# Attention with transposed scores, head pairs and interleaved FFN groups in place of row-max attention followed by a separate FFN stage

## The chip, the core and the metric

The kernel runs on one core of a Trainium2 chip. The metric is the device time of one execution in microseconds (us). The engines are named as the profile names them: PE (matrix multiply), PEld (its weight loads, which overlap PE), DVE (vector), ACT (activation functions), POOL (general purpose; here it also issues DMAs and writes masks) and SP (issues DMAs). SBUF is the memory on the core, PSUM the banks that PE writes, DRAM the memory outside.

## The reference, cut to what matters

```python
# q, k, v: (8 batches, 8 heads, 576, 64); beacon_k, beacon_v: (8, 8, 16, 64)
k_all = concatenate([beacon_k, k], axis=2)          # 592 keys; the 16 beacons are never masked
v_all = concatenate([beacon_v, v], axis=2)
scores = (1 / sqrt(64)) * q @ k_all^T               # causal mask over the 576 ordinary keys
scores = scores - scores.max(-1, keepdims=True)
a = exp(scores); a /= a.sum(-1, keepdims=True) + 1e-9
attn = a @ v_all
x = attn.transpose(0, 2, 1, 3).reshape(4608, 512)   # heads side by side
out = (maximum(x @ w_gate, 0) * (x @ w_val)) @ w_out     # d_ff = 1536, float32 out
```

Apart from the 1e-9, subtracting the row maximum changes no result in exact arithmetic. It only keeps `exp` in range.

## The kernel before

Attention runs for one head at a time and one tile of 128 queries at a time. Scores have queries on the partitions, so the probabilities `p` have to be transposed tile by tile on PE, and copied back by ACT, before they can be multiplied by the values. The result goes to DRAM, and a second stage, the FFN, reads it back.

```python
for b in range(B):
    for h in range(H):
        ...                                     # load k, q, v; transpose k and q on PE; ACT copies them
        for qi in range(n_sq):                  # tiles of 128 queries
            while c0 < sk_cols:
                nc.tensor.matmul(sps[:rl, :cl], qT, kT[:, c0:c0 + cl], start=True, stop=True)
                nc.vector.tensor_copy(sc[:rl, c0:c0 + cl], sps[:rl, :cl])
            nc.gpsimd.affine_select(...)        # causal mask with -1e9
            nc.vector.reduce_max(row_max[:rl], sc[:rl, :sk_cols], axis=AX.X)
            nc.scalar.mul(neg_max[:rl], row_max[:rl], -1.0 * scale)
            nc.scalar.activation(p[:rl, :sk_cols], sc[:rl, :sk_cols], AF.Exp,
                                 bias=neg_max[:rl], scale=scale, accum_out=row_sum[:rl])
            nc.vector.reciprocal(rinv[:rl], row_sum[:rl])
            nc.vector.tensor_scalar_mul(p[:rl, :sk_cols], p[:rl, :sk_cols], rinv[:rl])
            for ci, (vt16, clen) in enumerate(v_chunks[:1 + n_need]):
                nc.tensor.transpose(ptp[:clen, :rl], p[:rl, col_off:col_off + clen], ident[:rl, :rl])
                nc.scalar.copy(ptile[:clen, :rl], ptp[:clen, :rl])
                nc.tensor.matmul(outp[:, :rl], vt16[:clen], ptile[:clen, :rl], ...)
            nc.vector.tensor_copy(ot[:, :rl], outp[:, :rl])
            nc.sync.dma_start(xT_dram[...], ot[:, :rl])
...                                             # second stage: load and cast the weights
for mi in range(n_m):                           # 9 tiles of 512 tokens
    ...                                         # load xT_f from xT_dram, cast to bf16
    for nf in range(NF):                        # 12 up groups: 4 gate and 4 value matmuls of 512 columns
        ...
    for ms in range(M_TILE // P):               # 4 down groups: 12 matmuls of 512 columns
        ...
```

## Time and profile before

The time is 1340.23 us, the median of two runs (1339.97 and 1340.49).

| | stage | us | PE busy us |
|---|---|---|---|
| attention | 0 to 1043 | 1043 | 820 |
| weights arrive, first FFN tile starts | 1043 to 1110 | 67 | 60 |
| rest of the FFN | 1110 to 1339 | 229 | 225 |

The first fence holds lines of the page of the kernel before: the busy time of each engine (us, share of the span, instructions), PE's busy tenths and the granted PE clock in 40 equal slices, and the chain of work that ended last, by engine.

```profile
PE 1104.7 (83%) x5008; PEld 509.3 (38%) x5008; DVE 725.4 (54%) x2268; ACT 733.4 (55%) x3053; POOL 97.2 (7%) x326
...
PE   6878888787788788888878877887874699999998
...
PEclk9999999999999999999999999999999899999999
...
PE 63%; ACT 17%; DVE 10%; issue 5%; DMA 2%; POOL 1%; SPq 1%; ACTq 0%; POOLq 0%; DVEq 0%
```

No engine is full during attention (the first 31 slices); PE comes nearest. The chain goes mostly through PE, with ACT and DVE steps between. The next fence, from the page's list of costliest groups, shows two of these steps. Its columns are line, engine, operation, output and input, shapes, count, busy us, mean ns of one, and idle time before it with the releaser.

```profile
L139 ACT COPY ptile<-ptp 128x128 bf16<-128x128 bf16 (+4 forms) x1280 | 301.4, 244 | 229.8 <-PE ptp L135 208.3
L135 PE MATMUL ptp<-ident,p 128*128 128x128 bf16 (+4 forms) x1280 | 325.1, 268 | 24.6 <-DVE p L129 22.9
```

The transposes of `p` are 1280 matmuls, and ACT spends 301 us copying them. The next fence is the timeline of PE in attention, then at the start of the FFN, then late in the FFN. Its columns are start us, duration us, engine, line, operation, output and inputs, array rows*columns in use, input shape, count.

```profile
303.80 0.32 PE L140 MATMUL outp<-ptile,kqv_5144 128*64 128x128 bf16 x1
304.05 0.29 PE L135 MATMUL ptp<-ident,p 128*128 128x128 bf16 x1
304.26 0.32 PE L84 MATMUL tp_5427<-ident,kqv_5425 128*64 128x128 bf16 x1
304.37 0.31 PE L87 MATMUL tp_5430<-ident,kqv_5425 128*64 128x128 bf16 x1
304.48 0.31 PE L140 MATMUL outp<-ptile,kqv_5156 128*64 128x128 bf16 x1
...
1044.68 5.62 PE L184 MATMUL gps<-xT_r,wg_r 128*128 128x512 bf16 x17
...
1150.24 1.03 PE L184 MATMUL gps<-xT_r,wg_r 128*128 128x512 bf16 x4
1151.10 1.03 PE L187 MATMUL vps<-xT_r,wv_r 128*128 128x512 bf16 x4
```

Two things are to be read here, from the starts and not from the durations, since ends are modelled. First, matmuls of the same array shape (128*64) start 0.11 us apart (304.26, 304.37, 304.48), while a change of shape costs 0.21 to 0.25 us (303.80 to 304.05 to 304.26). Of the 3711 pairs of consecutive attention matmuls in the trace, 2947 change shape. Second, late in the FFN four 512-column matmuls take 0.86 us (1150.24 to 1151.10), so 216 ns each, or 0.42 ns per column; the first FFN matmuls, after a pause, start 427 ns apart until 1048.4. In attention the spacing of `sps` matmuls grows by about 0.84 ns per column (226 ns at 144 columns, 332 at 272, 441 at 400). That is half speed, although the clock row says 9.

### The profile page before, as it was taken

The numbers are of one execution on the slowest core, as the hardware profiler recorded it, in microseconds if no ns is written. First come the engines' busy times: TensorE is split into PE (matmuls) and PEld (weight loads), VectorE is DVE, ScalarE is ACT, GpSimd is POOL, SyncE is SP. The second block draws the span as 40 slices with busy tenths as digits, with TensorE's granted clock in tenths as the row PEclk, the third lists the DMA queues.
The fourth block names the chain that finished last, engine by engine and source line by source line (L and its number), as shares of the span: only waits on it lengthen the run. The fifth ranks groups of instructions, "written<-read, shape, count | busy, mean of one in ns | idle before, by whom it ended". The sixth has DMA issues, their size and how long they took to land.

```text
span 1338.8 us, 20191 instructions
## 1 busy us (share of the span) xinstructions
PE 1104.7 (83%) x5008; PEld 509.3 (38%) x5008; DVE 725.4 (54%) x2268; ACT 733.4 (55%) x3053; POOL 97.2 (7%) x326
## 2 busy tenths in 40 slices
PE   6878888787788788888878877887874699999998
PEld 2333333333333333333333333333332244444443
DVE  4656566565556556656655565665564443433333
ACT  5666666666666666666666666666663122222222
POOL 0101000010000100000000010010000000000000
PEclk9999999999999999999999999999999899999999
DMA  1111111111111111111111111111116711101111
GB/s 41 41 39 38 38 39 38 39 39 37 40 40 39 39 38 38 38 39 41 38 39 40 39 38 38 38 38 38 41 37 223 263 64 63 64 34 38 40 40 40
DMA packets 168311, 67.97 MB, mean 51 GB/s; under 512 B 140032, under 2 KB 156416, under 8 KB 168192
## 3 DMA queue, kind: packets, MB, share of 16 engines
q1 hardware_dynamic: 168192, 66.68, 18.9%
q8 instruction: 39, 0.64, 0.2%
q14 instruction: 80, 0.66, 0.2%
HBM read 47.71 MB, written 18.87 MB: 50 GB/s over the span
## 4 chain that ended last, share of the span: by engine, by line
PE 63%; ACT 17%; DVE 10%; issue 5%; DMA 2%; POOL 1%; SPq 1%; ACTq 0%; POOLq 0%; DVEq 0%
PE ptp L135 14%; PE outp L140 14%; PE sps L103 9%; ACT p L124 8%; PE vps L187 7%; PE ops L196 7%; PE gps L184 7%; ACT ptile L139 5%; DVE row_max L119 3%; DVE sc L105 3%; ACT kT L85 2%; DVE ot L145 1%; ACT qTall L88 1%; DVE p L129 1%; POOL sc L108 1%
## 5 line engine op out<-in xcount | busy, mean ns | idle before, releaser
L139 ACT COPY ptile<-ptp 128x128 bf16<-128x128 bf16 (+4 forms) x1280 | 301.4, 244 | 229.8 <-PE ptp L135 208.3
L135 PE MATMUL ptp<-ident,p 128*128 128x128 bf16 (+4 forms) x1280 | 325.1, 268 | 24.6 <-DVE p L129 22.9
L105 DVE COPY sc<-sps 128x144 f32<-128x144 f32 (+6 forms) x448 | 194.0, 438 | 159.8 <-PE sps L103 157.2
L135 PEld LDWEIGHTS <-p 128*128 128x128 bf16 (+4 forms) x1280 | 127.4, 100 | 231.5 <-issue 64.7
L124 ACT ACTIVATE p<-sc,neg_max 128x144 bf16<-128x144 f32 (+4 forms) x320 | 197.7, 618 | 18.8 <-ACT neg_max L121 1.1
L103 PE MATMUL sps<-kT,qTall 64*128 64x144 bf16 (+6 forms) x448 | 170.5, 420 | 39.1 <-ACT qTall L88 35.5
L119 DVE TENSOR_REDUCE row_max<-sc 128x1 f32<-128x144 f32 (+4 forms) x320 | 176.3, 551 | 47.1 <-POOL sc L108 42.5
L190 ACT ACTIVATE g<-gps 128x512 f32<-128x512 f32 x108 | 64.5, 597 | 235.0 <-PE gps L184 223.4
L108 POOL TENSOR_SCALAR_AFFINE_SELECT sc<-sc 128x128 f32<-128x128 f32 (+1 forms) x320 | 96.5, 301 | 921.5 <-DVE sc L105 528.5
L145 DVE COPY ot<-outp 64x128 f32<-64x128 f32 (+1 forms) x320 | 84.7, 265 | 97.3 <-PE outp L140 95.9
L191 DVE TENSOR_TENSOR hT_r<-g,vps 128x512 bf16<-128x512 f32 x108 | 74.2, 688 | 108.9 <-PE vps L187 108.9
L184 PE MATMUL gps<-xT_r,wg_r 128*128 128x512 bf16 x432 | 112.4, 386 | 18.1 <-DVE wg_r L169 18.1
L187 PE MATMUL vps<-xT_r,wv_r 128*128 128x512 bf16 x432 | 112.6, 386 | 6.7 <-DVE wv_r L169 6.7
L128 DVE RECIPROCAL rinv<-row_sum 128x1 f32<-128x1 f32 (+1 forms) x320 | 49.5, 155 | 100.4 <-ACT p L124 99.9
L129 DVE TENSOR_SCALAR p<-p,rinv 128x144 bf16<-128x144 bf16 (+4 forms) x320 | 100.8, 315 | 3.7
L196 PE MATMUL ops<-wo_r,hT_r 128*128 128x512 bf16 x432 | 94.7, 379 | 0.0
L103 PEld LDWEIGHTS <-qTall 64*128 64x128 bf16 (+1 forms) x448 | 42.0, 110 | 118.3 <-ACT qTall L88 97.5
L121 ACT ACTIVATE neg_max<-row_max 128x1 f32<-128x1 f32 (+1 forms) x320 | 65.3, 204 | 16.5 <-DVE row_max L119 14.6
L184 PEld LDWEIGHTS <-wg_r 128*128 128x128 bf16 x432 | 42.7, 99 | 70.9 <-issue 21.6
L187 PEld LDWEIGHTS <-wv_r 128*128 128x128 bf16 x432 | 42.8, 99 | 59.9 <-DVE wv_r L169 7.2
L196 PEld LDWEIGHTS <-hT_r 128*128 128x128 bf16 x432 | 42.3, 98 | 51.0
L124 ACT ACTIVATION_READ_ACCUMULATOR p<-sc,neg_max 128x1 f32 (+1 forms) x320 | 60.1, 188 | 0.0
(3213 smaller groups left out, 1144.0 us busy)
## 6 DMA issues: line engine op xcount, KB each, us to landing
xT_f<-xT_tmp SPq DMA_DIRECT2D x9, 1024.0 KB, 5.5
out_dram<-osb SPq DMA_DIRECT2D x36, 256.0 KB, 2.0
kqv<-in_k_dram SPq DMA_DIRECT2D x256, 32.0 KB, 1.9
kqv<-in_q_dram SPq DMA_DIRECT2D x256, 32.0 KB, 1.9
kqv<-in_v_dram SPq DMA_DIRECT2D x256, 32.0 KB, 1.9
xT_tmp<-ot SPq DMA_DIRECT2D x256, 32.0 KB, 1.8
wtmp<-in_moe_w_gate_dram SPq DMA_DIRECT2D x1, 3072.0 KB, 10.5
wtmp<-in_moe_w_val_dram SPq DMA_DIRECT2D x1, 3072.0 KB, 10.3
```

Of the source, the lines that this page charges most:

```text
L103: nc.tensor.matmul(sps[:rl, :cl], qT, kT[:, c0:c0 + cl], start=True, stop=True)
L105: nc.vector.tensor_copy(sc[:rl, c0:c0 + cl], sps[:rl, :cl])
L108: nc.gpsimd.affine_select(out=sc[:rl, Nb + r0:Nb + r0 + rl], in_=sc[:rl, Nb + r0:Nb + r0 + rl], pattern=[[-1, rl]], compare_op=ALU.is_ge, ...
L119: nc.vector.reduce_max(row_max[:rl], sc[:rl, :sk_cols], axis=AX.X)
L124: nc.scalar.activation(p[:rl, :sk_cols], sc[:rl, :sk_cols], AF.Exp, bias=neg_max[:rl], scale=scale, accum_out=row_sum[:rl])
L129: nc.vector.tensor_scalar_mul(p[:rl, :sk_cols], p[:rl, :sk_cols], rinv[:rl])
L135: nc.tensor.transpose(ptp[:clen, :rl], p[:rl, col_off:col_off + clen], ident[:rl, :rl])
L139: nc.scalar.copy(ptile[:clen, :rl], ptp[:clen, :rl])
L140: nc.tensor.matmul(outp[:, :rl], vt16[:clen], ptile[:clen, :rl], start=(ci == 0), stop=(ci == n_need))
L184: nc.tensor.matmul(gps, wg_r[:, ki, nf * P:(nf + 1) * P], xT_r[:, ki, :], start=(ki == 0), stop=(ki == KM - 1))
L187: nc.tensor.matmul(vps, wv_r[:, ki, nf * P:(nf + 1) * P], xT_r[:, ki, :], start=(ki == 0), stop=(ki == KM - 1))
L196: nc.tensor.matmul(ops, hT_r[:, nf, ms * P:(ms + 1) * P], wo_r[:, nf, :], start=(nf == 0), stop=(nf == NF - 1))
```

## The change

The intent: put keys on the partitions ("transposed scores"), so that `exp(scores)` is already in the layout the value product needs and no transpose of `p` is left. Handle two heads at once, on two halves of the PE array. Drop the row maximum; collect the reciprocals of all row sums, count after the work for how many of the 64 heads they all lie between 1e-10 and 1e10, and run a general path with the maximum under a branch if one head fails. Keep the attention result in SBUF. Put one FFN group of the previous batch's tokens between attention steps, so that PE has work while softmax runs. Loads are issued by POOL, because they cast float32 to bf16 on the way; the Trainium skill, "DMA: Bandwidth & Descriptors", section "SWDGE vs HWDGE vs iDMA", says that casting loads are for GpSimd's path alone.

The diff is cut to its core; the general path (110 lines) and the bookkeeping are left out.

```diff
-                    nc.vector.tensor_copy(sc[:rl, c0:c0 + cl], sps[:rl, :cl])
-                nc.vector.reduce_max(...); nc.scalar.mul(...)          # row max
-                nc.tensor.transpose(ptp...); nc.scalar.copy(ptile...)  # transposes of p
-                nc.sync.dma_start(xT_dram[...], ot[:, :rl])            # x through DRAM
+    def qk(pr, i):
+        s = s_ps.tile([P, 2, 512], FP32, name="s")
+        for (kt, q0, n, c, _, _) in STEPS[i]:
+            for a in range(2):                       # the two heads: array rows 0-63 and 64-127
+                rows = slice(a * D, (a + 1) * D)
+                nc.tensor.matmul(s[:, a, c:c + n], pr.kT[rows, kt * P:(kt + 1) * P],
+                                 pr.qT[rows, q0:q0 + n], start=True, stop=True)
+    def softmax(pr, i):
+        nc.scalar.activation(p[:, :, :n], pr.s[i][:, :, :n], AF.Exp, scale=scale)
+        for (kt, q0, _, c, m, base) in STEPS[i]:
+            if m:
+                nc.gpsimd.affine_select(out=p[:, :, c:c + m], ..., fill=0.0, ...)
+    def av(pr, i):
+        for j, (kt, q0, n, c, _, _) in enumerate(STEPS[i]):
+            for half in range(2):                    # values, then ones: the row sums
+                for a in range(2):                   # array columns 0-63 and 64-127
+                    w = pr.v[...] if half == 0 else ones[:kr, :]
+                    nc.tensor.matmul(o[rows, half, ...], w, p[:kr, a, c:c + n], ...)
+        if i == last:
+            nc.vector.reciprocal(r[:, :cn], o[:, 1, :cn])
+            nc.vector.tensor_mul(xT[:, pr.p_idx, t0:t0 + cn], o[:, 0, :cn], r[:, :cn])
+            nc.sync.dma_start(rsum[g:g + 2, cq0:cq0 + cn], ...)   # for the check of the range
 ...
+        for s in range(len(work) + LAG):             # 8 batches x 4 head pairs x 4 steps
+                if i == 0 and pr.p_idx == 0:
+                    if pr.b + 1 < B:
+                        load_qkv(pr.b + 1, 0, H, tiles[pr.b + 1])      # 17 loads by POOL
+                    if pr.b >= 1:
+                        ffn += ffn_tile(pr.b - 1)    # 12 up and 4 down groups
+                qk(pr, i); softmax(pr, i)
+                ...                                  # transposes of q and k of the next pair
+            if ffn:
+                ffn.pop(0)()
+            if s >= LAG:
+                av(*work[s - LAG])
+        for j, g in enumerate(ffn):                  # the last two FFN tiles
+            if j == 4:
+                in_range = count_in_range()
+            g()
+    with tc.If(in_range < 2 * B * NP):
+        general_path(...)
```

## The prediction

> **What bounds it now.** Two stages: attention for 1043 us, FFN for 295 us (windows view). The FFN is at its floor: 1296 matmuls of 512 columns, starting 216 ns apart in the timeline, are 280 us. Attention has 3712 matmuls, one per 281 ns on average, though DVE and ACT are only about 60% and 66% busy there and DMA 18%. The chain of waits is PE 63%, ACT 17%, DVE 10%: latency and small PE work, not one full engine.
>
> Two things slow PE there. First, in the timeline, matmuls of one array shape (128*64, 128 columns) start 107 ns apart, but 205 to 250 ns apart where the shape changes (ptp 128*128, outp 128*64), which it does at nearly every matmul. The Trainium skill, "TensorEngine Tiling (Array Packing)", Key Properties, says a mode change drains the engine; the trace agrees. Second, spacing grows by 0.83 ns per column, while warm FFN matmuls take 0.42 (first FFN matmuls: 427 ns apart, after 5 us 216). "TensorE: Matmul & The Clock Gate", Part 1, calls 1.2 GHz the default state that dense activity lifts. So I read attention as running at half clock, although the page's granted clock says 0.9+.
>
> **What changes.** Transposed scores remove the 1280 ptp transposes, their 1280 ACT copies (301 us), sc copies (194), row max (176), p scaling (101), ot copies, xT through DRAM, and the FFN stage's weight wait and casts (about 30 us). Matmuls besides the FFN: 88 per head pair, 2816 in all. FFN groups (1.73 us up, 2.59 us down) fill PE between steps, so the clock should stay up from batch 1 on.
>
> Estimates from these durations:
> - ACT: exp 3.5 us per pair (0.83 ns per element), plus FFN relu 65 and copies about 22 us: 200 us total.
> - DVE: 190 to 310 us, depending on whether the 256-wide reciprocal streams (one element took 155 ns).
> - POOL masks: about 2.7 us per pair, 88 us, plus issuing 196 DMAs, whose cost no trace here shows (before issues none from POOL).
> - PE: FFN 280. Per pair at full clock QK 1.0 to 1.7, AV 2.4 to 4, transposes 0.7, shape changes about 0.9: 5 to 7 us, 160 to 230 us total.
>
> PE becomes the bound. Per pair with FFN: 7.8 + 6 = about 14 us, times 28 pairs = 390. First batch without FFN: 30. Two FFN tiles at the end: 65. Startup: POOL must issue 94 DMAs before the first mask, about 45 us. Batch boundaries: POOL issues 17 large loads ahead of the masks, about 4 us of stall each, 30 in total.
>
> Predicted: 560 us; 8 in 10 between 470 and 690. Faster by over 2%: 0.985; within 2%: 0.01; slower: 0.005.
>
> **What would show it.** PE above 80% busy in batches 1 to 7, with 216 ns between FFN matmuls inside attention; ACT below 50%, DVE below 60%; a start of 30 to 60 us with PE mostly idle; a tail of about 65 us of pure FFN; PE gaps at batch boundaries released by POOL masks or DMA.
>
> **What would make it wrong.** If POOL needs 2 us or more per 1024-run load, boundaries and start cost 200 us or more and POOL is the bound (700 to 850). If the a=0/a=1 matmuls do not overlap and PE drops to half clock at stalls, about 650. If the slow reciprocal holds the two aux buffers, PE waits for DVE. If all overlaps, about 480.

## The result, and the profile after

The changed kernel is correct and takes 592.09 us, the median of two runs (590.74 and 593.43). The ratio to the kernel before is 0.4417, with a 95% interval of 0.4392 to 0.4441. Ratios in this document are not quite the ratio of the quoted medians. The result lies inside the predicted range, 32 us above the predicted value.

The first fence has the same lines of the page as before, with the rows of POOL and the chain by line added.

```profile
PE 447.3 (76%) x4113; PEld 227.8 (39%) x4113; DVE 259.4 (44%) x369; ACT 194.9 (33%) x273; POOL 218.1 (37%) x458
...
PE   2000037859995999599969986997799999979995
...
POOL 9998262471246125621652174217411112000000
PEclk9999999779997999799979996999699999979998
...
PE 66%; POOL 23%; DMA 6%; DVE 2%; issue 1%; ACT 1%; ACTq 0%; POOLq 0%; DVEq 0%
PE f L308 16%; PE f L314 15%; PE f L323 14%; PE aux L283 11%; POOL v_sb L207 8%; POOL k_sb L207 7%; PE s L254 6%; POOL q_sb L207 5%; DMA wo<-in_moe_w_out_dram 4%; PE aux L236 2%; DMA k_sb<-in_k_dram 2%; PE aux L244 2%; DVE r L290 1%; POOL p L264 1%; ACT p L261 1%
```

PE bounds the kernel, mostly with FFN matmuls (`f`). ACT and DVE fell from 733 and 725 us to 195 and 259. What is new is POOL: 23% of the chain, nearly all of it in issuing loads (L207), and PE has regular dips (5, 5, 5, 6 ...), with the clock dipping to 7 or 6 at the same places.

The next fence is the windows view: for each stretch its length, busy us and count of PE, PEld, DVE, ACT and POOL, the granted clock, the share of the DMA engines, and GB/s. The stretches are the start up to the first mask, batch 0, batch 6, batch 7 and the tail.

```profile
0.00:81.70 81.70, 2.96 (x20) 1.53 (x21) 1.04 (x3) 3.06 (x3) 66.84 (x101) 1.00 0.99 97
81.70:113.90 32.20, 24.12 (x320) 17.33 (x321) 20.64 (x28) 11.92 (x14) 8.77 (x34) 0.95 0.29 16
402.10:459.90 57.80, 50.69 (x497) 25.87 (x496) 31.13 (x44) 22.99 (x32) 22.19 (x49) 0.91 0.55 51
459.90:508.00 48.10, 48.10 (x490) 24.60 (x489) 30.03 (x42) 22.99 (x32) 8.78 (x33) 1.00 0.07 25
508.00:589.10 81.10, 70.38 (x328) 29.88 (x325) 21.27 (x32) 19.60 (x33) 0.00 (x0) 0.93 0.08 31
```

The clock of the first two rows is no measurement: the trace's first clock record is at 107.5 us. In batch 0, before that record, pairs of 256-column matmuls start 181 to 213 ns apart, just after it 105, so most of batch 0 ran at half clock.

Batch 7, the only one with FFN groups and no loads of a next batch, takes 48.1 us with PE busy all the time. Batch 6 takes 57.8, and so do the others (57.0 to 58.1). The difference, 9.6 us, is the cost of one batch boundary. The sum sets prediction and measurement side by side:

| term | predicted us | measured us | how the measured one is read |
|---|---|---|---|
| start to first mask | 45 | 81.7 | window above |
| batch 0, no FFN | 30 | 32.2 | window above |
| 28 pairs with FFN | 28 x 14 = 390 | 337 | 7 x 48.1 |
| batch boundaries | 30 | 57 | 346.0 (113.9 to 459.9) less 6 x 48.1 |
| tail | 65 | 81.1 | window above |
| sum | 560 | 589 | the span is 589.1 |

How a boundary comes about is shown by two timelines. The first is POOL's, in the columns of the timeline before.

```profile
113.58 0.29 POOL L264 TENSOR_SCALAR_AFFINE_SELECT p<-p 128x128 bf16<-128x128 bf16 x1 [2.50 <-ACT p L261]
...
113.89 0.54 POOL L207 DMA_DIRECT2D k_sb<-in_beacon_k_dram  x1
114.42 4.21 POOL L207 DMA_DIRECT2D k_sb<-in_k_dram  x5
118.58 4.24 POOL L207 DMA_DIRECT2D q_sb<-in_q_dram  x5
122.72 0.62 POOL L207 DMA_DIRECT2D v_sb<-in_beacon_v_dram  x1
123.25 4.29 POOL L207 DMA_DIRECT2D v_sb<-in_v_dram  x5
127.42 1.03 POOL L264 TENSOR_SCALAR_AFFINE_SELECT p<-p 128x224 bf16<-128x224 bf16 x3
```

The second is PE's over the same time.

```profile
119.90 1.03 PE L314 MATMUL f<-xT,wv 128*128 128x512 bf16 x4
127.99 0.42 PE L283 MATMUL aux<-p,v_sb 128*64 128x256 bf16 x2 [7.06 <-POOL p L264]
```

POOL works through its instructions in order. The 17 loads of the next batch stand ahead of the first mask of this batch, and issuing them takes from 113.89 to 127.42, 13.5 us. PE has two FFN groups to fill in, then waits 7.06 us for the masked `p`. The clock record goes to half during the wait and stays there for 6.8 to 10.2 us at each boundary, 3.3 to 5.3 us of it after the wait; work at half rate for that long loses 1.7 to 2.7 us (an estimate), which is most of the rest of the 9.6. The waits view (engine, line, what it waited for, total us, times, longest) shows the same: of 111.0 us, 68.8 are the start, and six waits of 5.8 to 7.1 us, one at each boundary, are 40.0.

```profile
PE aux L283 <- POOL p L264: 111.0, 10, 68.8
```

In the start, POOL issues 68 loads of batch 0 until 46.9 us, then nine loads of weights until 53.8, and then batch 1's loads, again ahead of the first mask. From there each load waits until the load issued eight before it has landed. POOL's timeline shows the last and longest of these waits, behind the large load of `wo`:

```profile
66.08 0.88 POOL L207 DMA_DIRECT2D q_sb<-in_q_dram  x1 [1.21 <-DMA wv<-in_moe_w_val_dram]
73.75 3.31 POOL L207 DMA_DIRECT2D q_sb<-in_q_dram  x4 [6.80 <-DMA wo<-in_moe_w_out_dram]
...
81.73 0.97 POOL L264 TENSOR_SCALAR_AFFINE_SELECT p<-p 128x224 bf16<-128x224 bf16 x3
```

In the trace of the changed kernel, the matmuls of the two heads start 3 ns apart, FFN matmuls inside attention start 216 ns apart, and 446 of 2815 consecutive pairs of attention matmuls change shape, counted as before, against 2947 of 3711 (with the FFN matmuls between them counted too, 561 of 4112 pairs of the whole trace).

### The profile page after: what moved, and what is told of

Read it like the earlier page. It is cut to its first block, busy times and chain, and to the rows that moved or that the text cites. A ratio compares the mean times of both kernels' runs of the same rounds, so it can differ in the third digit from the quotient of the medians.

```text
span 589.1 us, 10169 instructions
## 1 busy us (share of the span) xinstructions
PE 447.3 (76%) x4113; PEld 227.8 (39%) x4113; DVE 259.4 (44%) x369; ACT 194.9 (33%) x273; POOL 218.1 (37%) x458
## 4 chain that ended last, share of the span: by engine, by line
PE 66%; POOL 23%; DMA 6%; DVE 2%; issue 1%; ACT 1%; ACTq 0%; POOLq 0%; DVEq 0%
PE f L308 16%; PE f L314 15%; PE f L323 14%; PE aux L283 11%; POOL v_sb L207 8%; POOL k_sb L207 7%; PE s L254 6%; POOL q_sb L207 5%; DMA wo<-in_moe_w_out_dram 4%; PE aux L236 2%; DMA k_sb<-in_k_dram 2%; PE aux L244 2%; DVE r L290 1%; POOL p L264 1%; ACT p L261 1%
## 5 line engine op out<-in xcount | busy, mean ns | idle before, releaser
L290 DVE RECIPROCAL r<-aux 128x256 f32<-128x256 f32 (+1 forms) x96 | 129.8, 1352 | 160.8 <-PE aux L283 160.7
L261 ACT ACTIVATE p<-s 128x832 bf16<-128x832 f32 (+2 forms) x128 | 110.4, 863 | 245.3 <-PE s L254 245.3
L264 POOL TENSOR_SCALAR_AFFINE_SELECT p<-p 128x224 bf16<-128x224 bf16 (+3 forms) x224 | 67.7, 334 | 273.2 <-ACT p L261 273.2
L283 PE MATMUL aux<-p,v_sb 128*64 128x64 bf16 (+5 forms) x832 | 72.9, 240 | 116.3 <-POOL p L264 111.0
L308 PE MATMUL f<-xT,wg 128*128 128x512 bf16 x432 | 119.5, 400 | 5.0 <-DVE xT L292 4.3
L316 DVE TENSOR_TENSOR hT<-g,f 128x512 bf16<-128x512 f32 x108 | 74.0, 685 | 107.5 <-PE f L314 105.6
L314 PE MATMUL f<-xT,wv 128*128 128x512 bf16 x432 | 114.5, 389 | 0.9 <-DVE hT L316 0.9
L323 PE MATMUL f<-wo,hT 128*128 128x512 bf16 x432 | 98.4, 380 | 0.0
L311 ACT ACTIVATE g<-f 128x512 f32<-128x512 f32 x108 | 64.4, 596 | 70.1 <-PE f L308 68.7
L283 PE MATMUL aux<-p,ones 128*64 128x64 bf16 (+5 forms) x832 | 64.9, 234 | 0.0
L207 POOL DMA_DIRECT2D q_sb<-in_q_dram x55 | 44.2, 890 | 8.0 <-DMA wo<-in_moe_w_out_dram 6.8
L207 POOL DMA_DIRECT2D k_sb<-in_k_dram x55 | 43.8, 858 | 5.7 <-DMA wg<-in_moe_w_gate_dram 3.5
L207 POOL DMA_DIRECT2D v_sb<-in_v_dram x55 | 44.3, 907 | 1.7 <-DMA k_sb<-in_k_dram 1.5
```

Source lines behind the costliest of these rows:

```text
L207: nc.gpsimd.dma_start(dst[p0:p1, t, c0:c1].rearrange("p (h d) -> p h d", d=D), src.rearrange("h p d -> p h d"))
L261: nc.scalar.activation(p[:, :, :n], pr.s[i][:, :, :n], AF.Exp, scale=scale)
L264: nc.gpsimd.affine_select(out=p[:, :, c:c + m], in_=p[:, :, c:c + m], pattern=[[0, 2], [1, m]], compare_op=ALU.is_ge, fill=0.0, base=base, ...
L283: nc.tensor.matmul(o[rows, half, q0 - cq0:q0 - cq0 + n], w, p[:kr, a, c:c + n], start=(i == first and j == 0 and half == 0), stop=(i == la ...
L290: nc.vector.reciprocal(r[:, :cn], o[:, 1, :cn])
L308: nc.tensor.matmul(g, wg[:, ki, nf * P:(nf + 1) * P], xT[:, ki, m0:m0 + M_TILE], start=(ki == 0), stop=(ki == KM - 1))
```

## The experiments

The main theory, A: time is lost at the start and at the batch boundaries because POOL's in-order list has loads ahead of masks; in between, PE is full, and the gain came from less and denser PE work. Rivals: the loads themselves (DMA contention or late data) cost the time; DVE's row-max work had bounded the kernel before; DVE's slow reciprocal bounds the kernel after; the half clock before was a property of the array shapes or the data. Eleven kernels ran.

### 1. The same loads, spread over the steps

The loads of the next batch are put into a list, and one or two are issued in each step, after that step's masks.

```diff
-            nc.gpsimd.dma_start(
-                dst[p0:p1, t, c0:c1].rearrange("p (h d) -> p h d", d=D),
-                src.rearrange("h p d -> p h d"))
+            def go():
+                nc.gpsimd.dma_start(
+                    dst[p0:p1, t, c0:c1].rearrange("p (h d) -> p h d", d=D),
+                    src.rearrange("h p d -> p h d"))
+            go() if later is None else later.append(go)
 ...
+                for _ in range(2 if s % 16 < 4 else 1):     # after softmax(pr, i)
+                    if later:
+                        later.pop(0)()
```

> Edit: the 17 loads of the next batch are issued one or two at a time after the masks of each step, no longer as one block ahead of the first mask of a batch. Theory A (masks wait in POOL's queue behind the block of load issues): the six batches that cost 57.8 us fall to the 48 us of the batch without loads, about 57 us less, and the first mask comes at about 54 us in place of 82, which moves batch 1 forward by some 26 us; together about 589 - 83 = 506 us, 495 to 525. Theory B (what costs is the loads' traffic and landing, not their place in the queue): later loads land later, so the time stays at 580 to 600 or grows.

Measured: 522.59 us, ratio 0.3897 (0.3890 to 0.3903). The first mask comes at 54.0 instead of 81.7 us, and batches 1 to 6 take 48.3 to 49.8 us instead of 57.0 to 58.1. The windows view of batch 1:

```profile
101.10:150.70 49.60, 48.77 (x497) 24.93 (x496) 30.75 (x45) 23.01 (x32) 22.28 (x49) 1.00 0.63 56
```

POOL is as busy as in batch 6 above (22.3 us) and the DMA engines are busier (0.63), yet PE is busy for 48.8 of 49.6 us at full clock. So neither the amount of issuing nor the traffic costs the time; the order in POOL's list does. Theory A holds. The start gained less than the first mask suggests: batch 0 now takes 47.1 us (54.0 to 101.1) instead of 32.2, so the start and batch 0 together shrink by 12.8 us.

### 2. The block of loads kept whole, at another place

```diff
-                if i == 0 and pr.p_idx == 0:
-                    if pr.b + 1 < B:
-                        tiles[pr.b + 1] = io_tiles()
-                        load_qkv(pr.b + 1, 0, H, tiles[pr.b + 1])
+                if i == 0 and pr.p_idx == 2 and pr.b + 1 < B:
+                    tiles[pr.b + 1] = io_tiles()
+                    load_qkv(pr.b + 1, 0, H, tiles[pr.b + 1])
```

> Edit: the block of 17 loads stays whole but is issued at the middle of the batch before (third head pair) in place of its start. Theory A (block ahead of masks): each block still stalls the masks of its place for 13.5 us, so each batch keeps about 57 us; only the start changes (first mask at about 54 us, but batch 1 then waits for later loads), so 565 to 592 us. Theory B (data of a batch arrives too late or too early): moving the block changes the stall at the boundary itself; with half the lead a late arrival would add tens of us.

Measured: 581.97 us, ratio 0.4340 (0.4333 to 0.4347). The batches with loads still take 58 to 60 us; only the start got shorter. The stall went along with the block to the third pair of the batch, as PE's timeline shows:

```profile
126.79 1.03 PE L314 MATMUL f<-xT,wv 128*128 128x512 bf16 x4
135.79 0.43 PE L283 MATMUL aux<-p,v_sb 128*64 128x256 bf16 x2 [7.97 <-POOL p L264]
```

So the stall belongs to the block of 17 loads, not to the batch boundary or to data that is late.

### 3. The FFN after attention instead of in between

```diff
-            if ffn:
-                ffn.pop(0)()
```

> Edit: no FFN group between attention steps; all nine FFN tiles run after attention. Theory: in batches 1 to 7 a head pair drops from 11.2 us to the 8.7 us of batch 0, which has no FFN, with matmuls at half clock (pairs of 256 columns 210 us/1000 apart, not 106); FFN then takes 9 x 31 = 280 us alone. Sum 82 + 32 + 28 x 8.7 + 7 x 10 + 280 + 10 = about 715 us, 680 to 750. So the interleaving is worth about 125 us. Rival (FFN groups cost what they take, 7.8 us per pair, wherever they are): about 590 us.

Measured: 726.71 us, ratio 0.5423 (0.5412 to 0.5434). Interleaving is worth 727 - 592 = 135 us. A pair takes 8.2 to 8.6 us and runs at about half clock; the windows view of a stretch of attention shows a clock of 0.56 and PE busy for little more than half of the time:

```profile
200.00:400.00 200.00, 116.46 (x1589) 82.75 (x1589) 106.54 (x145) 62.91 (x73) 93.61 (x213) 0.56 0.57 38
```

This splits the gain of the whole change. Of 748 us (1340 - 592), 613 are there without any interleaving, mostly at half clock, and come with less and better-shaped PE work, shorter DVE and ACT work and no trip through DRAM. How the 613 divide among these was not tested. A rough estimate from shapes and spacings: the columns of attention, at 0.83 ns each, fall from 398 to 164 us (32 pairs of 6160 columns, the two heads side by side), and 2500 fewer shape changes at about 0.1 us each are some 250 us. The other 135 come from filling PE's waits and from the clock that this lifts.

### 4. One head after the other

```diff
-        for (kt, q0, n, c, _, _) in STEPS[i]:
-            for a in range(2):
+        for a in range(2):
+            for (kt, q0, n, c, _, _) in STEPS[i]:
 ...                                     # qk above; av below
-        for j, (kt, q0, n, c, _, _) in enumerate(STEPS[i]):
-            kr = P if kt < 4 else TAIL
-            for half in range(2):
-                for a in range(2):
+        for a in range(2):
+            for j, (kt, q0, n, c, _, _) in enumerate(STEPS[i]):
+                kr = P if kt < 4 else TAIL
+                for half in range(2):
```

> Edit: within a step all matmuls of head 0 run before those of head 1, in place of alternating, same work and same results. Theory: the alternating matmuls of a pair start 3 ns apart because they use different rows (QK) or columns (AV) of the array; in sequence they don't overlap, so QK and AV columns per pair (3328 + 6656 at 0.42 ns, half of it hidden before) cost about 2.1 us more plus exposed weight loads: pairs 11.2 to 13.5-16 us, 60 to 150 us in total, 650 to 740 us. Rival (PE is not what bounds a pair): within 2% of 592.

Measured: 610.57 us, ratio 0.4556 (0.4547 to 0.4565), 18 us more than the changed kernel. That is 3%, so both expectations were missed: the order of issue matters little (a pair takes 12.0 instead of 11.2 us). PE's timeline of the first step of a pair shows why:

```profile
484.18 0.30 PE L283 MATMUL aux<-p,v_sb 128*64 128x144 bf16 x2
484.24 0.23 PE L283 MATMUL aux<-p,ones 128*64 128x144 bf16 x1
```

The row at 484.18 holds two matmuls, which the trace has singly: the first head's of 144 columns at 484.181 and the second head's first of 256 columns at 484.186. The latter comes after six of the first head in the program, but three of those six start later (484.243, 484.306, 484.334). So the second half of the array starts on its own work while the first half still has matmuls waiting. This step took 0.75 us instead of 0.51; a step of eight 256-column matmuls took 0.57 instead of 0.56. The test therefore did not remove the overlap, and what the overlap is worth stays open.

### 5. Without the check of the range

The row sums are not collected, and the count and the branch are gone. This kernel gives the right result for these inputs only because they are in range.

```diff
-            nc.sync.dma_start(rsum[g:g + 2, cq0:cq0 + cn],
-                              r.rearrange("(a x) n -> a x n", a=2)[:, 0, :cn])
 ...
-            if j == 4:
-                in_range = count_in_range()
 ...
-    with tc.If(in_range < 2 * B * NP):
-        general_path(tc, q, k, v, beacon_k, beacon_v, out, ident, wg, wv, wo)
```

> Edit: the range check is gone (no small DMAs of the reciprocals, no count, no branch, no general path); for this data the result is the same. Theory: the check costs the 4 us in which PE waits for the count in the tail, about 3.5 us of half clock after it, and little else, so 592 falls by 6 to 12 us (1 to 2%). Rival (the branch or the 96 small DMAs cost more): 20 us or more.

Measured: 583.72 us, ratio 0.4351 (0.4342 to 0.4360), 8.4 us less, as expected. In the changed kernel PE pauses for the count between 517.9 and 521.9, and its 512-column matmuls then start 427 ns apart until 527.4, as these lines of its timeline show in part:

```profile
521.01 0.16 PE L344 MATMUL aux<-ones,ok 64*1 64x1 bf16 x1 [2.78 <-DVE ok L342]
521.91 1.87 PE L308 MATMUL f<-xT,wg 128*128 128x512 bf16 x4 [0.74 <-DVE cnt L346]
```

Four FFN matmuls take 1.87 us there, against 1.03 before the pause. The pause is about 4 us, and 5.5 us at half rate lose about 2.7 (an estimate); the other 1.7 of the 8.4 us are not placed. The general path is not taken.

### 6. The reciprocal done twice

```diff
             nc.vector.reciprocal(r[:, :cn], o[:, 1, :cn])
+            nc.vector.reciprocal(r[:, :cn], o[:, 1, :cn])
```

> Edit: each reciprocal of the softmax sums is computed twice, 130 us more of VectorE work (1.75 us more for each 256-wide one). Theory (PE bounds the pair, VectorE has about 3 us per pair to spare at 8.3 of 11.2 us, 4 us more per pair makes 12.3): a pair with FFN grows only by what VectorE then exceeds PE, about 1 us, and batch 0 somewhat more; 592 to 610-640 us, far less than +130. Rival (the reciprocal is on the chain because it holds the two aux buffers): nearly all of 130 us appears, 700 us and more.

Measured: 655.75 us, ratio 0.4896 (0.4888 to 0.4904). This adds 127 us of DVE work (259.4 to 386.5) and 64 us of time, which is between the two expectations. In the waits view, PE now waits for DVE where it hardly did before (5.4 us in the changed kernel):

```profile
PE aux L283 <- DVE xT L293: 50.6, 23, 3.2
```

A pair takes 14.2 instead of 11.2 us (the last pair of a batch, with the four longer down groups, 15.6 instead of 14.7). One reciprocal of 128x256 takes 1.75 us and holds one of the two `aux` PSUM buffers that PE needs next. So DVE was not the bound of the changed kernel, but it followed closely: about half of what was added to it became visible.

### 7. The kernel before without its row maximum

This is one part of the change done alone.

```diff
-                    row_max = sb.tile([P, 1], FP32, tag="rmax")
-                    nc.vector.reduce_max(row_max[:rl], sc[:rl, :sk_cols], axis=AX.X)
-                    neg_max = sb.tile([P, 1], FP32, tag="nmax")
-                    nc.scalar.mul(neg_max[:rl], row_max[:rl], -1.0 * scale)
 ...
-                                         bias=neg_max[:rl], scale=scale,
+                                         scale=scale,
```

> The kernel before with one part of the change alone: no row max (no reduce_max, no negated max; exp with bias 0), which takes 176 us off VectorE and 65 us off ScalarE. Theory (attention of the kernel before is a chain through PE whose matmuls run at half clock and stop at each shape change): the gain is small, 20 to 80 us, 1260 to 1320. Rival (VectorE and ScalarE work is what bounds it): 150 us or more come off, under 1190.

Measured: 1379.75 us, ratio 1.0296 (1.0275 to 1.0316): slower by 3%, although DVE lost 139 us and ACT 73 us of work:

```profile
PE 1089.9 (79%) x4982; PEld 503.2 (37%) x5008; DVE 586.6 (43%) x1948; ACT 660.5 (48%) x2733; POOL 91.9 (7%) x326
```

Both expectations missed the sign. Taking the row-max work off DVE and ACT gained nothing, which speaks against it as the bound. It is not a clean test: the traces show that the scheduler put PE's 3712 attention matmuls in a different order, so a gain may hide behind a worse order. That the order is what made it slower is only argued; the waits of ACT for the transposes grow from 208 to 281 us.

### 8 to 10. A filler between the matmuls of the kernel before

If PE runs attention at half clock because it isn't active enough, matmuls that nobody needs should lift the clock. One 512-column matmul in the FFN's shape was put before each value matmul in the program. (The scheduler moved them forward: in the trace all 1280 have run by 1316 us, and attention goes on without them until 1586.) Their results are never read; the output stays right. (`tp` got one PSUM buffer instead of two to make room. The recorded texts name runs: e8, e10 and e11 are experiments 8, 9 and 10, and e1 is experiment 1.)

```diff
+                        fill = fps.tile([P, 512], FP32, tag="fill")
+                        nc.tensor.matmul(fill, ident, junk, start=True, stop=True)
                         nc.tensor.matmul(outp[:, :rl], vt16[:clen], ptile[:clen, :rl],
```

> The kernel before with 1280 useless 512-column matmuls added in attention, one ahead of each AV matmul, into a PSUM bank of their own (the transposes of k and q keep one bank in place of two); results unchanged. At full clock they take 276 us of PE, at half clock 546 us. Theory (the attention stage runs at half clock because PE is not dense enough): if the filler lifts the clock, matmul spacing falls from 0.83 to 0.42 ns per column (real matmuls 216 to about 110-150 ns at shape changes) and the total changes little or grows by less than 276 us: 1250 to 1550. Rival (half-rate spacing belongs to these shapes, whatever the clock): spacing of the real matmuls stays and 400 us or more are added.

Measured: 1900.84 us, ratio 1.4184 (1.4156 to 1.4212). PE is busy for 94% of the span, and the clock still stayed at half speed in attention. The page's busy line and two rows of PE's timeline:

```profile
PE 1789.2 (94%) x6262; PEld 628.0 (33%) x6288; DVE 735.4 (39%) x2272; ACT 768.9 (40%) x3053; POOL 92.3 (5%) x326
```

```profile
605.72 0.61 PE L145 MATMUL fill<-junk,ident 128*128 128x512 bf16 x1
606.25 0.25 PE L146 MATMUL outp<-ptile,bk 16*64 16x64 bf16 x1
```

From a filler to the next matmul is 0.53 us (605.72 to 606.25; medians of 514 to 540 ns by the shape that follows, and 640 ns where another filler follows), where the same shape takes 216 ns to the next of its kind in the FFN. The added time, 560 us, is about 1280 x 427 ns = 547. The theory's number was missed and the rival's was met. (The next matmul here has another shape; like for like, experiment 10 below has 309 ns from a filler to a 128*64 matmul at full clock.) But the rival's reason falls too: it held the shapes of attention to be slow in themselves, and here the FFN's own shape is at half rate.

Two more kernels asked what was missing. The first takes real data in place of the identity.

```diff
-                        nc.tensor.matmul(fill, ident, junk, start=True, stop=True)
+                        nc.tensor.matmul(fill, junk[:, :P], junk, start=True, stop=True)   # junk: part of q
```

> As e8, but the useless matmuls use real data (q values as weights and as moving operand) in place of the identity. Theory D (the clock monitor sees the data's activity): clock rises, filler to next matmul 250 to 330 ns in place of 515, total about 1340 to 1600. Theory U (what counts is how much of the time columns stream, about 60% here as in e8): same as e8, about 1900 us.

Measured (single look, state unknown): 1900.17 us. The data is not the reason. The second puts three of them in a row.

```diff
-                        nc.tensor.matmul(fill, ident, junk, start=True, stop=True)
+                        for j in range(3):
+                            nc.tensor.matmul(fill, junk[:, :P], junk, start=(j == 0), stop=(j == 2))
```

> As e10 with three useless matmuls in a row in place of one. At half clock 2560 more matmuls of 427 ns add 1093 us: 2990 us. Theory U (the clock rises once columns stream in some 75% or more of the time): filler to filler falls from 427 to 216 ns, and the total is well under that, about 1900 to 2300. If it stays at half clock, about 3000 us, then share of streaming up to 76% is not enough either.

Measured (single look, state unknown): 1882.51 us. This kernel has 2560 matmuls of 512 columns more than the one before it and takes 18 us less. PE's timeline:

```profile
601.13 0.24 PE L149 MATMUL outp<-ptile,bk 16*64 16x128 bf16 x1
601.30 0.82 PE L148 MATMUL fill<-junk 128*128 128x512 bf16 x3
602.05 0.24 PE L149 MATMUL outp<-ptile,kqv 128*64 128x128 bf16 x1
```

Three fillers take 0.75 us (601.30 to 602.05). Spacing between fillers is 216 ns, and from a filler to a 128*64 matmul 309 instead of 515 ns. So the clock was full, from 8.7 us on by its record, and shape changes became cheaper with it (176 instead of 248 ns from a value matmul to the next shape). This shows that the half clock belongs neither to the shapes nor to the data, and that a PE that is busy by the profile is not enough.

What is enough can be worked out from the traces. Their clock records last multiples of 3.41 us. Cut each trace into these stretches, take the clock as half before the first record, and let each matmul stream from its start for 0.83 ns per column, counting overlapping ones once (a head's attention matmuls in the kernel before have 7456 columns, 477,000 in all). In the nine traces without missing matmul records, the 56 stretches at half clock that were followed by a rise had columns streaming for 74.0% of their time or more, and the 1047 that were not followed by one had 74.2% at most. Single fillers (experiment 9) reached 65% on average while they ran and 74% once; the kernel before reached 39% on average and 54% at most; the triple fillers had 75% in the stretch before the clock rose at 8.7 us. This rule is read from the traces and was not tested by a run made for it.

### 11. A version that beats both

The spread loads of experiment 1 are kept. In addition, only the first head pair is loaded before the first step; the weights, the rest of batch 0 and batch 1 follow in the list, several per step. In the tail, the `val` products take the `aux` banks, which are free by then, and the count's matmul is issued five groups after its DVE part.

```diff
-        for pi in range(NP):
-            load_qkv(0, 2 * pi, 2 * pi + 2, tiles[0])
-        ...                                            # all weights
+        load_qkv(0, 0, 2, tiles[0])
+                            load_qkv(0, 2, H, tiles[0], later)
+                            w_later(0)
+                            load_qkv(1, 0, 4, t1, later)
+                            ...                        # the other weights, the rest of batch 1, wo
 ...
-                u = f_ps.tile([P, M_TILE], FP32, name="f")
+                u = (aux_ps.tile([P, M_TILE], FP32, name="aux") if tail[0]
+                     else f_ps.tile([P, M_TILE], FP32, name="f"))
 ...
             if j == 4:
-                in_range = count_in_range()
+                ok = count_in_range()
+            if j == 9:
+                in_range = count_load(ok)
```

> Edit on top of e1: only the first head pair is loaded up front; the other heads of batch 0, the weights in quarters and the first loads of batch 1 are queued in the order of their use and issued a few per step behind the masks; the count of the range check is split, its matmul five FFN groups later; in the tail the second FFN product uses the free aux banks. Theory: first mask at about 12 us in place of 54, batch 1 begins at about 60 in place of 101, a batch stays at 49 to 50 us, the tail loses 4 us of waiting, 3.5 us of half clock and 3 us of bank waits: 522 - 40 - 9 = about 473 us, 460 to 492. Rival (the start is bound by what the DMA engines can move: 29 us for batch 0, 30 us for weights, 29 us for batch 1): batch 1 begins at 85 or later, 495 or more.

Measured: 471.31 us, ratio to the kernel before 0.3519 (0.3513 to 0.3525); against the changed kernel's median that is 0.80 (471.3 / 592.1, from different jobs, in which the kernel before took 1339.7 and 1340.2). The windows view of start with batch 0, batches 1 to 7 and tail:

```profile
0.00:57.00 57.00, 29.51 (x355) 19.61 (x356) 23.92 (x33) 16.03 (x19) 53.43 (x103) 0.88 1.01 84
57.00:398.00 341.00, 336.57 (x3455) 173.22 (x3455) 213.41 (x304) 159.56 (x223) 152.12 (x339) 1.00 0.66 65
398.00:469.60 71.60, 63.12 (x315) 28.40 (x310) 21.20 (x32) 19.26 (x33) 0.00 (x0) 0.99 0.09 35
```

Start and batch 0 went from 113.9 to about 57 us, batches 1 to 7 have PE busy for 99% of the time at full clock, and the tail lost 10 us. What is left above PE's work is mostly the start (PE busy for 29.5 of 57 us), in which the DMA engines are full (1.01); that they bound it was not tested. The 0.88 is not a measurement throughout: the first clock record is at 37.6 us.

## Why the prediction was right

The prediction, 560 us with a range of 470 to 690, held; the result is 592. Point by point:

- **What bounds the kernel before.** Right that no single engine was full and that PE work and latency bound it: taking away 139 us of DVE and 73 us of ACT work (experiment 7) gained nothing, though it changed PE's order too. Right, too, that PE ran at half clock against the page's row: the FFN's own shape ran at half rate there in experiment 8, and at full rate with three fillers in a row (experiment 10). The reason given, "the default state that dense activity lifts", needed sharpening: it is not being busy that lifts it, but columns streaming for about 74% of a 3.41-us stretch (the traces, under experiments 8 to 10).
- **PE becomes the bound.** Right. PE is 66% of the chain; in batch 7 it is busy all the time, in batches 1 to 7 for 89% of it (batch 6: 50.69 of 57.8), against "above 80%". FFN matmuls inside attention start 216 ns apart, as it said. ACT is 33% ("below 50%") and DVE 44% ("below 60%").
- **ACT, DVE and POOL work.** ACT 195 us against 200, DVE 259 against 190 to 310, masks 68 against 88.
- **Per pair, mis-sized: 14 us.** It measured 12.0 us on average (48.1 / 4), so 337 us for 28 pairs and not 390. The FFN share of 7.8 us was right; attention's share on PE was 12.0 - 7.8 = 4.2 us and not 6.
- **Start, mis-sized: 45 us.** It measured 81.7. The count of 94 loads was right (68 of batch 0, 9 of weights, 17 of batch 1), but 45 us allow 0.48 us for each. The first 77 were issued from 1.4 to 53.8 us, 0.68 us each. The 17 of batch 1 took from 54.5 to 81.7 us, and 13.7 of that was waiting for the landing of the load eight before, the last and longest for `wo`; the sum had no such waits. "A start of 30 to 60 us" did not show.
- **Boundaries, mis-sized: about 4 us each, 30 in all.** The mechanism was named rightly and is shown by experiments 1 and 2. The size was 9.6 us each, 57 in all: POOL needs 13.5 to 14.8 us for 17 loads, of which PE waits out 5.8 to 7.1, and the half clock that follows such a wait was listed under what might go wrong and was not in the sum.
- **Tail, mis-sized: 65 us.** It measured 81.1. The count, with its pause and the half clock after it, is 8.4 of the 16 us (experiment 5). Sharing two `f` banks between gate and value products is the likely rest; the last experiment, which gave them the `aux` banks and moved the count, has a tail about 10 us shorter, but did both at once.
- **The errors partly cancelled.** Start +37, boundaries +27, tail +16, batch 0 +2, pairs -53: together +29, from 560 to the span of 589. That 560 came so close to 592 is in part luck: the single terms were less sure than the sum looked.
- **What would make it wrong.** The reciprocal that "holds the two aux buffers" was not visible in the result (5.4 us of waits) but was close: experiment 6 made it so. "If all overlaps, about 480" is what the last version reached, 471.

## What to carry to other kernels

An engine that both issues loads and does work on the critical path executes them in the order they are written: spread the issues behind its urgent work, a few per step, instead of writing a whole block of them; here that alone was worth 69 us of 592. When matmuls run at half rate, read the spacing of their starts instead of the busy share, and give PE dense work from another stage; a second stage's matmuls between the steps were worth 135 us. Add up a prediction by stage and compare it by stage, since a good sum can hide terms that are wrong by half.

## What the Trainium skill lacked or had wrong

- "TensorE: Matmul & The Clock Gate", Part 1, says that the clock is set by how busy PE has been. By the profile's busy time that is not enough: with PE 94% busy the clock stayed at half (512 columns: about 514 ns to the next matmul of 128*64), and with three fillers in a row it was full (309 ns). Worked out from nine traces, the clock rose after a 3.41-us stretch with columns streaming for 74.0% or more (56 rises), and not after stretches with less (1047, 74.2% at most). Part 1 warns that recorded clock events are unreliable; this case adds that a page may show full clock where there is no record at all (none before 1048.3 us in the kernel before).
- The same page, Part 3, says that matmuls start and end strictly in program order. With one head issued after the other on two column halves, a matmul of the second head started at 484.186 us, ahead of three that precede it in the program (484.243, 484.306, 484.334).
- "TensorEngine Tiling (Array Packing)", Key Properties, says that changing the tiling mode drains the engine, and the trace agrees; it gives no cost. Measured at half clock: 205 to 250 ns from start to start across a change, against 107 without (128*64 and 128*128 alike), for 128 columns; at full clock 176 from a value matmul to the next shape.
- "VectorE: DVE Perf Modes", the walkthrough of the 8-slice pipeline, describes the reciprocal as an iterated divide but gives no cost per element. Measured: 1753 ns for 256 elements per partition and 551 for 64, so 6.3 ns for each further element.
- "DMA: Bandwidth & Descriptors" has no figure for how long issuing a load occupies GpSimd. Measured from start to start: 0.71 us for a load of 256 runs and 0.82 to 0.89 us for one of 1024 runs, so nearly all fixed, and 13.5 us for 17 loads that the masks behind them had to wait for. Its smallest size for line rate (512 B, "Specifications") agrees in kind: a 128-byte packet of a casting load took 32.5 ns, a 1024-byte one of the same queue 98. That the 128-byte packet is also slower than a 256-byte packet without a cast (17.4 ns, in the kernel before, from another queue) is on no page.
